# Last layer of a float32 kernel: two of three output tiles by Strassen's scheme, weights stationary

## The chip, the cores and the metric

The kernel runs on one core of a Trainium2 chip. The metric is device time of one execution in microseconds (us), the median of several runs. The engines are named as in the profile: PE (TensorE matmuls), PEld (its weight loads), DVE (VectorE), ACT (ScalarE), POOL (GpSimd), SP (the queue that issues most DMAs).

## The reference

```python
def _moe_ref(x, w1, w2, w3, w_out):
    a = x @ w1
    b = x @ w2
    h = a * b @ w3
    return (h @ w_out).astype(np.float32)
...
def _moe2_ref(x, w_in, w_out):
    h = x @ w_in
    relu6 = np.clip(h + 3.0, 0.0, 6.0)
    g = h * relu6 / 6.0
    return (g @ w_out).astype(np.float32)
...
    attn_out = _attn_ref(**attn_kwargs)
    x = attn_out.transpose(0, 2, 1, 3).reshape(B * S, H * D)
    x = _moe_ref(x=x, **moe_kwargs)
    return _moe2_ref(x=x, **moe2_kwargs)
```

There are 3072 tokens. The width is 384, the first feed-forward part has 1024 hidden units, the second 2048. The attention part is a recurrence with a decaying state. The weights come in as 64-bit floats, the rest as 32-bit floats.

## The kernel before

The tokens go in NB = 6 blocks of TB = 512. Attention units of two heads each come first and run beside the first feed-forward part; its w3 and w_out are folded into one matrix ahead of time, so that it has two layers. Call the products with w1 and w2 layer 1 (`l1_a`, `l1_b`, L720 to L734), the folded product layer 2 (`l2`, L737), the product with w_in layer 3 (`l3`, L804) and the product with the last w_out layer 4 (`l4`, L830).

Every large product is made of three float32r matmuls (`mm3`, L153 to L156): each operand is split into a rounded part hi and a remainder lo, and the sum is hi·hi + hi·lo + lo·hi. `split` (L149) makes the two parts: a copy on ACT (L150), a subtraction on POOL (L151).

In layers 3 and 4 the loop `steps2` runs over 6 blocks and, in each, over NM2 = 16 tiles m of 128 hidden units: 96 steps. A step issues on PE nine matmuls of layer 3 for tile m, 512 tokens moving (weights of w_in stationary), and then twelve of layer 4 for the tile before: for each of NC = 4 groups of 128 tokens, three matmuls with the tokens stationary and the 384 outputs moving, added into four PSUM banks over the block's 16 tiles. Between them stands the activation: DVE makes t = max(h+3, 0) (L811) and g = min(t, 6)·h (L817), ACT copies g to ghi (L150), POOL subtracts to glo (L151). At a block's end the four banks are scaled by 1/6 and written out as rows of 384 (L866, L870, L874).

The weights of layers 3 and 4 are read as 64-bit words and converted to 32 bits by a stream (`ws2`): two ACT instructions (L77, L78) and two DVE instructions (L85, L89) for a tile of 128x384, then `split`. `CONV` and `CONV2` say how many tiles are converted in each step: before, 18 in the last nine steps of layers 1 and 2, the rest one per step in the first block of layer 3. `u`, the first of the two words, lies in PSUM in the first part (`ws2.banks`) and in SBUF afterwards.

A check on alpha (`load_dev`, `deviate`, `make_flag`, `flag_sum`) is spread over some steps; its flag decides whether a general path runs at the end, which it doesn't here.

Up to step 46 of layers 1 and 2 a scheduler orders the instructions; from there (`MANUAL_FROM`) each engine runs them in the order of the code.

## Time and profile before

| | |
|---|---|
| median of 3 runs (range) | 880.73 us (879.99 to 882.34) |
| the profiled execution's own time | 878.07 us |
| its span, first to last instruction | 876.3 us |
| PE busy | 858.2 us (98% of the span), 6206 matmuls |
| DVE, ACT, POOL busy | 463.7, 344.5, 372.4 us |
| mean granted TensorE clock | 0.998 |

The first layer-3 matmul starts at 462.2 us, the last layer-4 matmul at 867.9 us: nearly half of the span is the stage that the change rewrites. A busy PE counts matmuls whose recorded times overlap; the pace is read from the distance between starts.

### The profile page before, as it was taken

To read this page: it belongs to the slowest core of one execution; us is meant where nothing else is said; L and a number is where in the kernel's file an instruction comes from. 1 tells how busy PE (TensorE), PEld (TensorE's weight loads), DVE (VectorE), ACT (ScalarE), POOL (GpSimd) and SP (SyncE) were. 2 spreads that over 40 slices of the span, in tenths; PEclk is the share of its full clock that TensorE was granted. 3 is DMA by queue.
4 is the path that set the end of the run, shared out by engine and by line. 5 is a ranking of instruction groups with operands and counts; after the bars stand their busy time and mean duration, and the time that the engine had idled before them with its cause. 6 is when DMAs were issued, how large, how long until landed. Compare 5 with 4: busy or idle time off the path is not lost.

```text
span 876.3 us, 16309 instructions
## 1 busy us (share of the span) xinstructions
PE 858.2 (98%) x6206; PEld 733.3 (84%) x6206; DVE 463.7 (53%) x838; ACT 344.5 (39%) x760; POOL 372.4 (42%) x388
## 2 busy tenths in 40 slices
PE   6999999999999999999999999999999999999996
PEld 5777888888888888888788999999899999999995
DVE  6787767887776767623426563333333333333332
ACT  4777776333322332326735465444221122121111
POOL 1445546334443334356545573342253243343231
PEclk9999999999999999999999999999999999999999
DMA  8896564376354443105523334022001001001001
GB/s 201 229 234 198 146 176 91 50 126 93 59 100 67 94 62 60 55 21 190 179 58 126 128 112 141 1 76 70 1 12 61 1 13 61 1 13 37 0 1 41
DMA packets 185127, 74.18 MB, mean 85 GB/s; under 512 B 154704, under 2 KB 173520, under 8 KB 185040
## 3 DMA queue, kind: packets, MB, share of 16 engines
q1 hardware_dynamic: 182336, 69.70, 32.4%
q0 software_dynamic: 2560, 3.15, 1.3%
q8 instruction: 51, 0.84, 0.4%
q14 instruction: 36, 0.29, 0.1%
q10 hardware_dynamic: 144, 0.20, 0.1%
HBM read 58.85 MB, written 9.44 MB: 78 GB/s over the span
## 4 chain that ended last, share of the span: by engine, by line
PE 93%; DMA 2%; ACT 1%; DVE 1%; issue 1%; POOL 0%; SPq 0%; POOLq 0%; DVEq 0%; ACTq 0%
PE acc L843 23%; PE h L154 8%; PE h L155 8%; PE h L156 7%; PE w L154 7%; PE w L156 7%; PE w L155 7%; PE acc L743 4%; PE acc L744 4%; PE acc L746 4%; PE sc L371 2%; PE facc L154 1%; PE facc L156 1%; PE facc L155 1%; PE py L458 1%
## 5 line engine op out<-in xcount | busy, mean ns | idle before, releaser
L151 POOL TENSOR_TENSOR glo<-g,ghi 128x512 fp32r<-128x512 f32 x95 | 125.7, 1323 | 234.0 <-ACT ghi L150 231.1
L811 DVE TENSOR_SCALAR t<-h 128x512 f32<-128x512 f32 x96 | 66.4, 692 | 232.3 <-PE h L156 232.3
L150 ACT CAST ghi<-g 128x512 fp32r<-128x512 f32 x95 | 59.0, 621 | 274.1 <-DVE g L817 252.8
L843 PE MATMUL acc<-wo2hi,ghi 128*128 128x384 f32 x384 | 130.3, 339 | 0.0
L843 PE MATMUL acc<-wo2lo,ghi 128*128 128x384 f32 x384 | 130.1, 339 | 0.0
L151 POOL TENSOR_TENSOR ablo<-ab,abhi 128x512 fp32r<-128x512 f32 x48 | 63.9, 1332 | 129.6 <-ACT abhi L150 129.5
L154 PE MATMUL w<-xhi,w 128*128 128x512 f32 x288 | 115.1, 401 | 1.6 <-ACT asb L723 1.4
L155 PE MATMUL h<-ylo,wihi 128*128 128x512 f32 x288 | 113.9, 395 | 0.0
L154 PE MATMUL h<-yhi,wihi 128*128 128x512 f32 x288 | 113.7, 395 | 0.0
L156 PE MATMUL w<-xhi,w 128*128 128x512 f32 x288 | 113.1, 393 | 0.0
L155 PE MATMUL w<-xlo,w 128*128 128x512 f32 x288 | 112.5, 391 | 0.0
L156 PE MATMUL h<-yhi,wilo 128*128 128x512 f32 x288 | 111.9, 388 | 0.0
L843 PE MATMUL acc<-wo2hi,glo 128*128 128x384 f32 x384 | 83.7, 339 | 0.0
L843 PEld LDWEIGHTS acc<-wo2hi,ghi 128*128 128x128 f32 x384 | 72.0, 188 | 5.1 <-ACT yt L756 0.8
L843 PEld LDWEIGHTS acc<-wo2lo,ghi 128*128 128x128 f32 x384 | 72.0, 188 | 3.5
L85 DVE SCALAR_TENSOR_TENSOR w<-u,w 128x384 uint32<-128x384 uint32 (+1 forms) x72 | 51.9, 724 | 40.5 <-ACT w L78 23.8
L817 DVE SCALAR_TENSOR_TENSOR g<-t,h 128x512 f32<-128x512 f32 x96 | 66.0, 688 | 9.9 <-POOL glo L151 0.2
L843 PEld LDWEIGHTS acc<-wo2hi,glo 128*128 128x128 f32 x384 | 69.1, 188 | 0.0
L154 PEld LDWEIGHTS w<-xhi,w 128*128 128x128 f32 x288 | 54.1, 188 | 14.2 <-ACT asb L723 1.8
L156 PEld LDWEIGHTS h<-yhi,wilo 128*128 128x128 f32 x288 | 54.1, 188 | 12.8
L156 PEld LDWEIGHTS w<-xhi,w 128*128 128x128 f32 x288 | 54.1, 188 | 11.6
L155 PEld LDWEIGHTS w<-xlo,w 128*128 128x128 f32 x288 | 54.1, 188 | 10.3
(131 smaller groups left out, 1507.7 us busy)
## 6 DMA issues: line engine op xcount, KB each, us to landing
raw<-in_moe_w_out SPq DMA_DIRECT2D x24, 384.0 KB, 3.3
raw<-in_moe_w SPq DMA_DIRECT2D x16, 512.0 KB, 4.9
raw<-in_moe_w SPq DMA_DIRECT2D x16, 384.0 KB, 3.5
raw<-in_moe_w_in SPq DMA_DIRECT2D x16, 384.0 KB, 3.7
y<-yt SPq DMA_DIRECT2D x18, 256.0 KB, 3.5
yraw<-y SPq DMA_DIRECT2D x18, 256.0 KB, 2.8
dev<-in_alpha SPq DMA_DIRECT2D x24, 192.0 KB, 3.7
out<-ot SPq DMA_DIRECT2D x23, 192.0 KB, 2.0
```

The source lines that it names most:

```text
L85: nc.vector.scalar_tensor_tensor(out=low, in0=u.bitcast(U32), scalar=3, in1=low, op0=ALU.logical_shift_left, op1=ALU.bitwise_or,)
L150: nc.scalar.copy(out=hi, in_=x)
L151: nc.gpsimd.tensor_tensor(out=lo, in0=x, in1=hi.bitcast(F32), op=ALU.subtract)
L154: nc.tensor.matmul(out=dst, lhsT=lh, rhs=rh, start=start, stop=False)
L155: nc.tensor.matmul(out=dst, lhsT=lh, rhs=rl, start=False, stop=False)
L156: nc.tensor.matmul(out=dst, lhsT=ll, rhs=rh, start=False, stop=stop)
L743: nc.tensor.matmul(out=acc1[o], lhsT=wh[:, sl], rhs=hi, start=m == 0, stop=False)
L744: nc.tensor.matmul(out=acc1[o], lhsT=wl[:, sl], rhs=hi, start=False, stop=False)
L746: nc.tensor.matmul(out=acc1[o], lhsT=wh[:, o * P:(o + 1) * P], rhs=lo, start=False, stop=m == NM1 - 1)
L811: nc.vector.tensor_scalar(out=t, in0=ps, scalar1=3.0, scalar2=0.0, op0=ALU.add, op1=ALU.max)
L817: nc.vector.scalar_tensor_tensor(out=g, in0=t, scalar=6.0, in1=ps, op0=ALU.min, op1=ALU.mult)
L843: nc.tensor.matmul(out=acc2[o], lhsT=x[:, o * P:(o + 1) * P], rhs=y, start=m == 0 and x is hi and y is wh, stop=stop,)
```

## The change

Layer 4 is done for pairs of tiles m. For outputs 0 to 255 (two tiles of 128) a pair's contraction (two tiles of 128), the two output tiles and the two halves of 256 tokens make a 2x2 by 2x2 product, done with seven products of blocks instead of eight. The third output tile (`o0`, `o1`) stays as it was. Weights are now stationary and tokens move: 256 columns in the seven products, 512 in the third tile. A pair issues on PE 7·3 matmuls of 256 columns and 2·3 of 512, where two steps before issued 24 of 384. The sums and differences of weights are made once (`pair_ops`); those of tokens are made in each pair (`operands`), with the subtraction for lo on DVE, and the combination of the seven sums into outputs once a block (`drain`). The outputs lie with output units on partitions, so that they are turned: on DVE in 32x32 blocks, and written in pieces of 128 bytes (`put_out`), in the last block on PE (`put_last`). The activation's first half goes from DVE to ACT as a Relu with bias 3. Conversion is moved: 26 weight tiles in the last nine steps of layers 1 and 2, six later, and five are loaded earlier. The check on alpha is taken later and more widely spaced.

```diff
-CONV = (2, 2, 2, 2, 2, 2, 2, 2, 2, 0)
-CONV2 = (0, 1)
+CONV = (5, 4, 3, 3, 3, 3, 3, 2, 0, 0)
+CONV2 = (0, 1, 1, 0, 0, 0, 0, 1, 1, 1, 1)
+HT = TB // 2
+NPAIR = NM2 // 2
+FIRST = (3, 6, 4, 7)
+SECOND = (2, 1, 5)
+PLACE = {3: (0, 0), 6: (0, 1), 4: (1, 0), 7: (1, 1), 2: (2, 0), 1: (2, 1), 5: (3, 0)}
+ONPOOL = ()
+DRAIN = ({2: (2, 1)}, {0: (3,), 1: (5, 0)})
+PUT = {3: 2, 4: 0, 5: 1}
...
+    def pair_ops(p, x0, x1):
...
+        nc.vector.tensor_tensor(
+            out=de[:, 0:2].rearrange("p o n -> p (o n)"), in0=col(x1, 0, 2), in1=col(x0, 0, 2), op=ALU.subtract
+        )
+        nc.vector.tensor_tensor(out=de[:, 2], in0=col(x0, 0), in1=col(x0, 1), op=ALU.add)
+        nc.vector.tensor_tensor(out=de[:, 3], in0=col(x1, 0), in1=col(x1, 1), op=ALU.add)
+        nc.vector.tensor_tensor(out=de[:, 4], in0=col(x0, 0), in1=col(x1, 1), op=ALU.add)
...
+            split(t[:, :, 0], t[:, :, 1], src)
...
+            (0, (4, 3, 6), de[:, 0:3]), (1, (7, 1), de[:, 3:5]),
+            (2, (5, "o1"), x1[:, P:].rearrange("p (o n) -> p o n", o=2)),
+            (3, (2, "o0"), x0.rearrange("p (o n) -> p o n", o=3)[:, ::2]),
...
+        g = ph2.tile([P, TB], F32, tag="g", name="g", bufs=2)
+        nc.scalar.activation(out=g, in_=ps, func=AF.Relu, bias=three)
+        nc.vector.scalar_tensor_tensor(out=g, in0=g, scalar=6.0, in1=ps, op0=ALU.min, op1=ALU.mult)
+        gs[j, m] = g
+
+    def operands(j, m):
...
+        nc.vector.tensor_tensor(out=d, in0=g[:, HT:], in1=g[:, :HT], op=ALU.subtract)
...
+            nc.vector.tensor_tensor(out=sm, in0=g0, in1=g, op=ALU.add)
...
+            nc.vector.tensor_tensor(out=cr, in0=g0[:, :HT], in1=g[:, HT:], op=ALU.add)
...
+        for k, hi, lo, x in todo:
+            nc.scalar.copy(out=hi, in_=x)
+        for k, hi, lo, x in todo:
+            eng = nc.gpsimd if k in ONPOOL else nc.vector
+            eng.tensor_tensor(out=lo, in0=x, in1=hi.bitcast(F32), op=ALU.subtract)
...
+        if what == 0:
+            mm(b[:, 0], hi, (p, half) == (0, 0) and k != "o1", False)
+            mm(b[:, 1], hi, False, False)
         else:
+            mm(b[:, 0], lo, False, p == NPAIR - 1)
...
+    def l4a(p, then=None):
+        for k in FIRST + ("o0",):
+            prod(p, k, 0)
...
+        for k in FIRST + ("o0",):
+            prod(p, k, 1)
+
+    def l4b(p, groups=(SECOND + ("o1",),)):
+        for ks in groups:
+            for what in range(2):
+                for k in ks:
+                    prod(p, k, what)
...
+            scaled(oth["m3"], 3, -1)
+            scaled(oth["m4"], 4, 1)
+            gather(1, 1, 6, 1, oth["m3"])
+            gather(0, 0, 7, -1, oth["m4"])
+        elif what == 5:
+            gather(1, 0, 5, 1, oth["m3"])
+            gather(0, 0, 5, -1)
+        elif what == 2:
+            gather(0, 1, 2, 1, oth["m4"])
+            gather(1, 1, 2, -1)
+        elif what == 1:
+            gather(0, 0, 1, 1)
+            gather(1, 1, 1, 1)
         else:
...
+            scaled(oth[2], "o1", 1)
...
+        nc.vector.transpose(out=t, in_=x)
...
+    def put_last(j, cs_):
+        for c in cs_:
+            ps = ps_mm.tile([P, DM], F32, tag="mm", name="oT")
+            for o in range(KD):
+                nc.tensor.transpose(ps[:, o * P:(o + 1) * P], oth[o][:, c * P:(c + 1) * P], ident)
+            t = raw2.tile([P, DM], F32, tag="raw", name="ot", bufs=RAW2)
+            if c % 2:
+                nc.vector.tensor_copy(out=t, in_=ps)
+            else:
+                nc.scalar.copy(out=t, in_=ps)
...
+        jp, mp = divmod(j * NPAIR + m // 2 - 1, NPAIR)
+        if jp >= 0:
+            if m % 2:
+                l4b(mp)
+            else:
+                l4a(mp, flag_sum if si == FLAG + 2 else None)
+        if j:
+            for what in DRAIN[0].get(m, ()):
+                drain(j - 1, what)
+            if m in PUT:
+                put_out(j - 1, PUT[m])
+        operands(j, m)
+        chore(CHORES)
+        if j:
+            for what in DRAIN[1].get(m, ()):
+                drain(j - 1, what)
...
+    l4a(NPAIR - 1)
+    drain(NB - 1, 3)
+    l4b(NPAIR - 1, ((2, 1), ("o1", 5)))
+    for what in (0, 2, 1, 5):
+        drain(NB - 1, what)
+    put_last(NB - 1, range(NC // 2, NC))
+    put_last(NB - 1, range(NC // 2))
```

PE in the middle of the stage. Before, layer 4 of one tile, behind nine matmuls of layer 3 (`acc` are the four token groups):

```order
L843 MATMUL acc_6113<-wo2hi,ghi 128x384
L843 MATMUL acc_6113<-wo2lo,ghi 128x384
L843 MATMUL acc_6114<-wo2hi,ghi 128x384
L843 MATMUL acc_6114<-wo2lo,ghi 128x384
...
L843 MATMUL acc_6115<-wo2hi,glo 128x384
L843 MATMUL acc_6116<-wo2hi,glo 128x384
```

PE of the changed kernel, the first half of layer 4 of a pair (`l4a`) and, behind nine matmuls of layer 3, its second half (`l4b`); m_6306, m_6311, m_6351 and m_6356 are banks of the seven sums, m_6316 is the third output tile, `bop` the prepared weights:

```order
L952 MATMUL m_6306<-ghi,bop 128x256 x2
L952 MATMUL m_6306<-dd,bop 128x256 x2
L952 MATMUL m_6311<-ghi,bop 128x256 x2
L952 MATMUL m_6311<-dd,bop 128x256 x2
L952 MATMUL m_6316<-ghi,bop 128x512 x2
L952 MATMUL m_6306<-glo,bop 128x256
...
L952 MATMUL m_6351<-shi,bop 128x256 x2
L952 MATMUL m_6351<-cross,bop 128x256 x2
L952 MATMUL m_6356<-shi,bop 128x256 x2
L952 MATMUL m_6316<-ghi,bop 128x512 x2
L952 MATMUL m_6351<-slo,bop 128x256
```

All products with hi stand ahead of all with lo in each half, and the operands of the second half (`shi`, `cross`) are asked for one layer-3 tile later than those of the first.

DVE of the changed kernel, two steps in the middle of a block, where two steps before had four instructions (t, g, t, g); d is the difference of a tile's two token halves, sm the sum of the pair's two tiles, cr the sum of one half of each:

```order
L899 SCALAR_TENSOR_TENSOR g<-g,h 128x512
L910 TENSOR_TENSOR d<-g 128x256
L932 TENSOR_TENSOR glo<-g,ghi 128x512
L932 TENSOR_TENSOR dd<-d,dd 128x256
L899 SCALAR_TENSOR_TENSOR g<-g,h 128x512
L910 TENSOR_TENSOR d<-g 128x256
L918 TENSOR_TENSOR sm<-g 128x512
L922 TENSOR_TENSOR cr<-g 128x256
L932 TENSOR_TENSOR glo<-g,ghi 128x512
L932 TENSOR_TENSOR dd<-d,dd 128x256
L932 TENSOR_TENSOR slo<-sm,shi 128x512
L932 TENSOR_TENSOR cross<-cr,cross 128x256
```

Twelve instructions stand in two steps, and the four remainders of an odd tile are the last work ahead of the next tile's g.

## Rows read from the trace of the kernel before

**Rows 1.** The page: busy times of the engines, PE and its clock in 40 slices.

```profile
PE 858.2 (98%) x6206; PEld 733.3 (84%) x6206; DVE 463.7 (53%) x838; ACT 344.5 (39%) x760; POOL 372.4 (42%) x388
...
PE   6999999999999999999999999999999999999996
...
PEclk9999999999999999999999999999999999999999
```

**Rows 2.** Waits of PE: who, for whom, us in total, times, longest.

```profile
PE aT L313 <- DMA al<-in_alpha: 4.4, 1, 4.4
PE kb L406 <- DVE KT L360: 2.4, 1, 2.4
PE w L154 <- ACT asb L723: 1.4, 1, 1.4
```

**Rows 3.** Busy time by windows: stretch, length, PE, PEld, DVE, ACT, POOL, clock, DMA.

```profile
407.00:462.00 55.00, 53.59 (x237) 44.06 (x236) 21.58 (x39) 32.73 (x68) 30.61 (x29) 1.00 0.44 135
462.00:868.00 406.00, 405.97 (x2029) 367.06 (x2027) 157.44 (x233) 124.98 (x250) 163.05 (x128) 1.00 0.14 45
```

**Rows 4.** Timeline of PE, one step: start, length, what.

```profile
702.24 0.40 PE L154 MATMUL h<-yhi,wihi 128*128 128x512 f32 x1
...
704.32 0.34 PE L843 MATMUL acc<-wo2hi,ghi 128*128 128x384 f32 x1
...
706.44 0.40 PE L154 MATMUL h<-yhi,wihi 128*128 128x512 f32 x1
```

**Rows 5.** Timeline of PE, the first steps of the stage.

```profile
462.18 0.39 PE L154 MATMUL h<-yhi,wihi 128*128 128x512 f32 x1
...
464.22 0.39 PE L743 MATMUL acc<-abhi,w34hi 128*128 128x512 f32 x1
...
466.26 0.39 PE L154 MATMUL h<-yhi,wihi 128*128 128x512 f32 x1
...
470.99 0.39 PE L154 MATMUL h<-yhi,wihi 128*128 128x512 f32 x1
```

**Rows 6.** Groups by line of PEld, layer 4: count, busy us, mean ns.

```profile
L843 PEld LDWEIGHTS acc<-wo2hi,ghi 128*128 128x128 f32 x384 | 72.0, 188 | 5.1 <-ACT yt L756 0.8
```

**Rows 7.** Timeline of PEld where two loads meet no running float32r matmul.

```profile
290.81 0.19 PEld L743 LDWEIGHTS acc<-abhi,w34hi 128*128 128x128 f32 x1
290.92 0.19 PEld L744 LDWEIGHTS acc<-abhi,w34lo 128*128 128x128 f32 x1
```

**Rows 8.** Groups by line and form of DVE and ACT: durations by size.

```profile
L817 DVE SCALAR_TENSOR_TENSOR g<-t,h 128x512 f32<-128x512 f32 x96 | 66.0, 688 | 9.9 <-POOL glo L151 0.2
L524 DVE TENSOR_TENSOR A<-sb,low 128x256 f32<-128x256 f32 x32 | 11.2, 392 | 5.6 <-PE sb L518 5.6
L307 DVE STREAM_TRANSPOSE kT<-kn 128x512 f32<-128x512 f32 x15 | 10.3, 686 | 0.0
L824 DVE TENSOR_TENSOR glo<-g,ghi 128x512 fp32r<-128x512 f32 x1 | 0.7, 693 | 0.7 <-ACT ghi L823 0.7
L150 ACT CAST ghi<-g 128x512 fp32r<-128x512 f32 x95 | 59.0, 621 | 274.1 <-DVE g L817 252.8 <-PE acc L843 15.4 <-DVE flag L901 3.6
```

**Rows 9.** Timeline of DVE, t and g of one step.

```profile
704.52 0.69 DVE L811 TENSOR_SCALAR t<-h 128x512 f32<-128x512 f32 x1 [2.72 <-PE h L156]
705.31 0.69 DVE L817 SCALAR_TENSOR_TENSOR g<-t,h 128x512 f32<-128x512 f32 x1
```

**Rows 10.** Groups by line of POOL from 405 to 463 us.

```profile
L151 POOL TENSOR_TENSOR ablo<-ab,abhi 128x512 fp32r<-128x512 f32 x10 | 13.0, 1297 | 19.1 <-ACT abhi L150 19.1
L151 POOL TENSOR_TENSOR wilo<-w,wihi 128x384 fp32r<-128x384 f32 x11 | 11.2, 1025 | 9.5 <-ACT wihi L150 9.4
```

**Rows 11.** Timeline of DVE and POOL around 463 us.

```profile
461.63 0.56 DVE L89 SCALAR_TENSOR_TENSOR w<-u,w 128x384 uint32<-128x384 uint32 x1
...
463.12 2.32 POOL L151 TENSOR_TENSOR wilo<-w,wihi 128x384 fp32r<-128x384 f32 x2
...
463.13 1.43 DVE L85 SCALAR_TENSOR_TENSOR w<-u,w 128x384 uint32<-128x384 uint32 x1 [0.94 <-ACT w L78]
```

**Rows 12.** Timeline of the end, and four transposes on PE earlier.

```profile
115.94 0.60 PE L683 MATMUL w3ps<-cs,w 128*128 128x128 f32 x4
...
867.78 0.49 ACT L870 ACTIVATE ot<-acc 128x384 f32<-128x384 f32 x1 [0.57 <-PE acc L843]
867.94 0.33 PE L843 MATMUL acc<-wo2hi,glo 128*128 128x384 f32 x1
...
868.31 0.56 DVE L866 TENSOR_SCALAR ot<-acc 128x384 f32<-128x384 f32 x1 [0.50 <-PE acc L843]
```

More of the change, by code (lines that the diff above doesn't have):

```diff
@@ L144, in attn_moe_kernel @@
     nc.gpsimd.memset(adev, -ADEV * ADEV)
+    three = const.tile([P, 1], F32, tag="three", name="three")
+    nc.gpsimd.memset(three, 3.0)
     over = const.tile([P, NDEV], F32, tag="over", name="over")
@@ L165, in __init__ @@
             self.banks = []
+            self.spare = None
+            self.sent = self.made = 0
         def issue(self, count=1):
@@ L184, in prep @@
                         u = cv.tile([P, n], F32, tag="u", name="u", bufs=UB)
-                    w = cv.tile([P, math.prod(shape[1:])], F32, tag="w", name="w", bufs=WB)
+                    pl, bufs = cv, WB
+                    if self.spare and self.made < SPARED and self.made % (WB + 1) == WB:
+                        pl, bufs = self.spare, 1
+                    self.made += 1
+                    w = pl.tile([P, math.prod(shape[1:])], F32, tag="w", name="w", bufs=bufs)
                     f64_prep(nc, raw, u, w)
@@ L787, in attn_moe_kernel, with chore @@
+    chores = []
+    spread = []
+    def chore(n):
+        for _ in range(min(n, len(chores))):
+            f, *args = chores.pop(0)
+            f(*args)
     yraw = {}
@@ new lines, in attn_moe_kernel, with region, prod, mm @@
+    acc2 = {}
+    oth = {}
+    def region(k):
+        if k in PLACE:
+            i, half = PLACE[k]
+            return acc2[i][:, half * HT:(half + 1) * HT]
+        return acc2[4]
+    def prod(p, k, what):
+        i, half = PLACE.get(k, (4, 0))
+        if (p, what, half) == (0, 0, 0) and k != "o1":
+            pl, tag = ((ps_mm2, "mm2a"), (ps_mm2, "mm2b"), (ps_acc, "acc0"), (ps_acc, "acc1"), (ps_acc, "acc2"))[i]
+            acc2[i] = pl.tile([P, TB], F32, tag=tag, name=f"m{i}", bufs=1)
+        hi, lo = aop[k]
+        b = bop[p, k]
+        def mm(x, y, start, stop):
+            nc.tensor.matmul(out=region(k), lhsT=x, rhs=y, start=start, stop=stop, skip_group_check=True)
+        if what == 0:
+            mm(b[:, 0], hi, (p, half) == (0, 0) and k != "o1", False)
+            mm(b[:, 1], hi, False, False)
+        else:
+            mm(b[:, 0], lo, False, p == NPAIR - 1)
@@ L817, in l3, with scaled, gather @@
+    SIXTH = 1.0 / 6.0
+    def scaled(dst, k, sign):
+        nc.scalar.activation(out=dst, in_=region(k), func=AF.Copy, scale=sign * SIXTH)
+    def gather(o, t, k, sign, base=None):
+        dst = oth[o][:, t * HT:(t + 1) * HT]
         nc.vector.scalar_tensor_tensor(
-            out=g, in0=t, scalar=6.0, in1=ps, op0=ALU.min, op1=ALU.mult
-        )
-        ghi = gpool.tile([P, TB], F32R, tag="abhi", name="ghi")
-        glo = gpool.tile([P, TB], F32R, tag="ablo", name="glo")
-        if last:
-            nc.scalar.copy(out=ghi, in_=g)
-            nc.vector.tensor_tensor(out=glo, in0=g, in1=ghi.bitcast(F32), op=ALU.subtract)
-        else:
-            split(ghi, glo, g)
@@ new lines, in gather @@
+            out=dst, in0=region(k), scalar=sign * SIXTH, in1=dst if base is None else base,
+            op0=ALU.mult, op1=ALU.add,
+        )
+    def l4a(p, then=None):
+        for k in FIRST + ("o0",):
+            prod(p, k, 0)
+        if then:
+            then()
+        for k in FIRST + ("o0",):
[5 more added lines that the diff above has]
+                    prod(p, k, what)
@@ new lines, in put_out @@
+    def put_out(j, o):
+        x = oth.pop(o)
+        t = raw2.tile([P, TB], F32, tag="raw", name="oT", bufs=RAW2)
+        nc.vector.transpose(out=t, in_=x)
+        t = blocks(t)
+        for c, n, b, t0 in spans(j):
+            rows = out[b * S + t0:b * S + t0 + n * P, :].rearrange("(t r) d -> r t d", r=Q32)
+            for a in range(P // Q32):
+                d0 = o * P + a * Q32
+                nc.sync.dma_start(
+                    out=rows[:, :, d0:d0 + Q32],
+                    in_=t[a * Q32:(a + 1) * Q32, c * (P // Q32):(c + n) * (P // Q32), :],
+                )
@@ L898, in flag_sum @@
     def flag_sum():
-        pf = ps_mm2.tile([P, 2], F32, tag="mm2", name="pf")
-        nc.tensor.matmul(out=pf[:1, :1], lhsT=far[:, 1:2], rhs=ones[:, 0:1], start=True, stop=True)
-        nc.vector.tensor_copy(out=flag, in_=pf[:1, :1])
+        pf = ps_mm2.tile([P, TB], F32, tag="acc3", name="pf")[:1, :1]
+        nc.tensor.matmul(out=pf, lhsT=far[:, 1:2], rhs=ones[:, 0:1], start=True, stop=True)
+        nc.scalar.copy(out=flag, in_=pf)
     def w3_items(f):
@@ L971, in attn_moe_kernel @@
         if si == n1:
+            spare.close()
+            ph2 = pool(main, "ph2", 1)
             l3(*steps2[0])
```

251 lines of the change are left out of this document (140 added, 111 removed).

## The prediction, made blind

> **What bounds the kernel now.** I read the page first, then the waits of PE, the windows, and the timeline of one step. PE is busy in all but the first of 40 slices at the full clock level, 2.4 GHz, and its waits add up to some 10 us in three large pieces, all of them early [rows 1, 2]. So the kernel is as long as PE's list of work, and a change pays if it shortens that list without making PE wait. In the stage of layers 3 and 4, 462 to 868 us, PE is busy 405.97 of 406.00 us, while DVE has work for 157, ACT for 125 and POOL for 163 [rows 3]: there is room on DVE and ACT, and the change uses it.
>
> The pace of PE is the distance between starts, not the printed length. One step is 4.20 us (702.24 to 706.44): nine matmuls of 512 columns take 2.08, 231 ns each, and twelve of 384 take 2.12, 176.8 ns each [rows 4]. The difference is 54.2 ns for 128 columns, near the 53.3 that 128 columns take at 2.4 GHz, so some 15 ns a matmul do not depend on the columns. At the stage's start nine of the same 512-column matmuls took 2.04 us, 226.7 ns each [rows 5].
>
> **The change, part by part.** The times are against the profiled execution, 878.07 us with a span of 876.3.
>
> *Layer 4 on PE.* A pair of tiles costs now 24·176.8 = 4.243 us. It will cost 21 matmuls of 256 columns and 6 of 512. No row has a float32r matmul of 256 columns. Taking the column step once more off, 176.8 − 54.2 = 122.6 ns; the pair is 21·0.1226 + 6·0.231 = 3.961 us, 0.282 less, and 48 pairs make −13.6 us. The bounds are the weight load's. From below: two loads that meet no running float32r matmul follow each other after 0.11 us [rows 7], so a matmul with its own load is not paced under some 111 ns: −0.25 us a pair more, −25 us in all. From above: a load is printed with 188 ns [rows 6]; if the next matmul waited for that, a pair would cost 5.33 us, +52 us. I take 122.6: the 384-column matmuls already start 176.8 ns apart, under the 188 of the load between them, so the printed length is not a barrier, and 122.6 is still above 111.
>
> A rule speaks against the change here. The Trainium skill, page "TensorE: Matmul & The Clock Gate", section "The mechanism", says that a weight load overlaps matmuls in flight only where the row groups differ; all loads here use all rows. By that a 256-column matmul would cost its stream and a load of 107 ns (same page, "LDWEIGHTS (loading the stationary operand)"), well over 200 ns, and the stage would get longer by some 80 us, an estimate. The trace disagrees: 384 columns are 160 ns at 2.4 GHz and start 176.8 ns apart with a load each [rows 4], which leaves no room for a load in series.
>
> *DVE in a pair.* From the code it has twelve instructions: six of 512 columns at 0.69 us (two g, the sum, three remainders; the remainder's own row is 693 ns) and six of 256 at 0.392 [rows 8]: 6.49 us of a pair's 18·0.231 + 3.961 = 8.12. On PE this costs nothing while it is covered. What covers it: the remainders glo and dd of an odd tile are asked for by the second pass of `l4a`, which starts after nine layer-3 matmuls (2.08) and ten of the first pass (1.44), so 3.5 us after `l4b` let their buffers go; they need 1.1 us of DVE, so DVE may be 2.4 us late before PE waits. ACT does two Relus, three casts of 512 (0.621 each) and three of 256; at 0.69 or less each this is under 5 us of 8.12.
>
> *Combining a block's sums.* For five blocks DVE has eight more instructions of 256 columns and three transposes of 512 (0.686): 8·0.392 + 3·0.686 = 5.2 us [rows 8], within the next block's steps 0 to 5. Two pairs have 2·1.63 = 3.3 us to spare, so DVE falls back by 1.9, less than the 2.4 above. A block as a whole is covered (57.1 of 64.9 us). I take 0.2 us a block, 1 us in all; the bounds are 0 and 5·1.9 = 9.5. The outputs' many small writes go through SP's queue in the next block's first steps, ahead of that block's y loads, which are wanted three steps later: nothing.
>
> *The last block.* Nothing follows to cover it. Now the last matmul starts at 867.94, DVE starts on its output 0.37 later and is done after 0.56 [rows 12]. In its place come, behind the last product, two DVE instructions of 256 (0.70 at the pitch that overlaps their ends), three transposes at 0.11 (four took 0.60 with the last one's end [rows 12]), a copy of 0.5, and the same again for the second two groups, as only two PSUM banks hold transposed tiles: 0.37 + 0.70 + 2·(0.33 + 0.2 + 0.5) + 0.5, some 3.6 us in place of 0.93: +2.7. The last pair's operands come with no pair of work between: +0.5 (0 to 1.5).
>
> *Conversion moved.* From 407 us on POOL will do, by the order of the changed program, 14 splits of w_in, 6 of three and 18 of two tiles of prepared weights, ten ablo, one xlo, three ylo: at 1.025 and 1.297 us, and 0.75 for 256 columns by the same slope [rows 10], 52 us, in the 58 us until layer 2 asks for the last ablo. Then there are 24 sums and differences of weights on DVE, each with two SBUF operands. Where DVE ran such an instruction beside a POOL subtraction it took 1.43 us, not 0.56 [rows 11]; if POOL in turn is held for theirs (0.28 us on average), POOL comes to 59 us. So PE will wait in this stretch, for ablo or asb: 1 us at least, and with POOL's idle time of today (9.5 us behind wilo's casts [rows 10]) 10 at most. I take the middle, 5.4, less the 1.4 that PE waits there today [rows 2]: +4. The page "SBUF — State Buffer" of the Trainium skill, section "SBUF: two separate sides", says that VectorE instructions with two SBUF inputs and GpSimd lock each other out for a whole instruction; the row of 1.43 us agrees.
>
> *The first block.* Now the second step takes 4.73 us instead of 4.20 [rows 5]. Six weight tiles and the pipeline's filling remain: +0.5 (0 to 3).
>
> Sum: −13.6 + 1 + 2.7 + 0.5 + 4 + 0.5 = −4.9, so 873.2 us for the profiled execution. That one was 2.7 us under the median of its three runs; for the median this is 880.73 − 4.9 = 875.8 us, in round numbers **876**. About 0.3%, 2.6 us, is what a measurement of this kernel can tell from no change.
>
> **The rivals.**
>
> *The short matmul is cheaper.* If the stage ran as at its start, 226.7 ns for 512 columns and 118 for 256, a pair of steps would cost 7.92 us in place of 8.40: −22.8 + 8.7 = −14, 867 us. For: the first nine matmuls of the stage ran so [rows 5]. Against: every later step is at 231.
>
> *The weight load sets the pace (slower).* It has 111 of 122.6 ns. Each nanosecond over the latter costs 21·48 = 1.0 us, so at 127.5 ns the gain is gone, and from 130 the change is measurably slower. If the matmul gets no shorter than the 384-column one, 176.8 ns, it is 930 us. For: the margin is 11 ns, and today's matmuls show 15 ns that do not belong to columns. Against: 384 and 512 differ by what their columns take, so no load binds at 384.
>
> *DVE becomes the bound (slower).* If every instruction also waits 0.10 us for the one before, as g does behind t (0.79 from start to start, 0.69 long [rows 9]), a pair costs 7.69 us, five blocks with their 6.3 us more overrun by 2.9 us each, the first with its conversions by 5: +20 in place of 1.5, 894 us. It decides from some 7.5 us a pair. Against: most of the twelve do not depend on their neighbour.
>
> *The conversion stretch is worse.* With 10 to 14 us of waiting it is 881 to 886.
>
> **How the numbers follow.** My forecast 0.47, with its own range 869 to 883; cheaper matmul 0.15; load as the pace 0.15; DVE 0.10; conversion 0.13. Faster by over 0.3% (under 878.1): 0.36 + 0.15 + 0.01 = 0.52. Within: 0.10 + 0.05 + 0.01 = 0.16. Slower: 0.32. The range leaves out the load's case and a little of DVE's and goes from 863, a little under the cheaper matmul, to 893.
>
> **What would show it.** In the changed profile, starts of 256-column matmuls 122 to 124 ns apart and PE busy through the stage would bear out the main term; 130 or more refutes it. Waits of layer 4 for glo, dd, slo or cross on DVE would be the DVE rival; waits of layer 1 or 2 for asb or ablo between 407 and 466 us the conversion. The end should show about 3.6 us from the last product to the last copy. The forecast is wrong if PE waits in most pairs, or if the pace of layer 3 changes too.

## The result and the profile after

| | before | after |
|---|---|---|
| median (range), us | 880.4 (879.99 to 882.34) | 866.7 (865.26 to 870.25) |
| ratio, 95% interval | | 0.985 (0.982 to 0.989) |
| profiled execution, its span, us | 878.07, 876.3 | 870.25, 868.4 |
| mean granted clock | 0.998 | 0.991 |

The changed kernel is faster by 1.5%, 13.7 us in the medians, where 4.9 were forecast. The two profiled executions are only 7.8 us apart, and the trace tells why. PE's page rows of the changed kernel (to be read against [rows 1]):

```profile
PE 847.0 (98%) x6362; PEld 708.4 (82%) x6362; DVE 662.2 (76%) x1310; ACT 485.0 (56%) x1068; POOL 258.8 (30%) x310
...
PE   6999999999999999999899999999999999999996
...
PEclk9999999999999999999999999999999999999998
```

DVE has 662 us of work in place of 464, PE 11 us less. Three stretches of this execution ran at half the clock, 1.2 GHz. The windows around them (stretch, length, PE busy, clock, DMA share, GB/s):

```profile
27.00:30.40 3.40, 3.40 (x29) 0.51 1.03 246
143.10:146.50 3.40, 3.40 (x13) 0.50 0.01 1
433.30:436.70 3.40, 3.40 (x10) 0.50 0.67 233
```

Each costs half of its length, 1.7 us. The first two lie ahead of the stretches that were rewritten, and ahead of the early loads of weights, which are issued from 147.3 us on. A matmul of layer 1 that the kernel before starts at 405.40 us starts here at 408.61, so 3.2 us of this execution's time are counted apart from the change. `fourth_buffer`, with the same instructions there, had neither of the two stretches; whether the change makes them likelier is not shown. The kernel before had no such stretch in its profiled execution until PE's work was over.

Now the waits of PE in the changed kernel, against [rows 2]:

```profile
PE aT L340 <- DMA al<-in_alpha: 4.5, 1, 4.5
PE w L169 <- DVE ab L756: 2.9, 2, 2.4
...
PE m L952 <- ACT dd L929: 0.8, 2, 0.6
```

New are the two waits of layer 1 behind `ab` (1.4 us behind `asb` before) and small ones of layer 4 for its operands, in the first block. The windows, as in [rows 3] (PE, PEld, DVE, ACT, POOL, clock, DMA share, GB/s):

```profile
407.00:469.00 62.00, 59.08 (x252) 48.07 (x251) 45.71 (x80) 47.93 (x108) 49.19 (x50) 0.97 0.49 156
...
509.00:535.00 26.00, 24.92 (x133) 20.89 (x132) 23.88 (x47) 16.10 (x35) 7.13 (x7) 1.00 0.01 2
535.00:850.00 315.00, 315.00 (x1781) 275.74 (x1780) 266.16 (x534) 202.90 (x417) 15.50 (x12) 1.00 0.18 39
```

From 535 to 850 us PE is never idle, with DVE at 266 of 315 us. One pair of steps in that stretch, to be read against [rows 4] (start, length, what; x2 is two instructions in one row):

```profile
558.87 0.40 PE L169 MATMUL h<-yhi,wihi 128*128 128x512 f32 x1
...
560.93 0.40 PE L952 MATMUL m<-ghi,bop 128*128 128x256 f32 x2
561.16 0.40 PE L952 MATMUL m<-dd,bop 128*128 128x256 f32 x2
...
563.03 0.39 PE L169 MATMUL h<-yhi,wihi 128*128 128x512 f32 x1
...
565.07 0.40 PE L952 MATMUL m<-shi,bop 128*128 128x256 f32 x2
...
566.82 0.40 PE L169 MATMUL h<-yhi,wihi 128*128 128x512 f32 x1
```

Two 256-column matmuls start every 0.23 to 0.24 us; of the 815 neighbours of that size 791 are less than 130 ns apart, that is outside waits, and their mean distance is 117.6 ns. Layer 3 takes 2.06 and 2.04 us, and the pair 7.95 in place of 8.40. A whole block of eight pairs shows it with all that recurs in one, combining and transposes included:

```profile
547.12 0.39 PE L169 MATMUL h<-yhi,wihi 128*128 128x512 f32 x1
...
610.89 0.39 PE L169 MATMUL h<-yhi,wihi 128*128 128x512 f32 x1
```

That is 63.77 us for eight pairs, 7.97 each. With 48 pairs and the other places, the account of the two profiled executions is:

| place | forecast, us | trace, us | read from |
|---|---|---|---|
| pairs of steps | -13.6 | -20.6 | 48·(8.40 - 7.97) |
| combining | +1 | 0 | PE idle 0 from 535 to 850; one step is longer by 0.3 beside the flag's matmul, as one was before (622.15 to 626.66) |
| conversion stretch | +4 | +3.4 | stage starts at 468.83 (462.18 before), less 3.2 from earlier |
| first block | +0.5 | +3.7 | four first passes of layer 4 longer by 1.2, 1.9, 0.4, 0.7, less 0.5 of before [rows 5] |
| last pair's operands | +0.5 | +0.7 | its first pass took 2.75 us, not 2.10 |
| the end | +2.7 | +1.5 | last product to end of span 9.87 us, 8.36 before [rows 12] |
| half clock and waits before 407 us | | +3.2 | 408.61 against 405.40 |
| sum | -4.9 | -8.1 | 870.25 - 878.07 = -7.8; a hundredth in the pair's difference is worth 0.5 |

The 7.8 and the 3.2 counted apart give the change 11.0 us. The medians are 13.7 apart: the 7.8 of these two executions, the 2.3 by which that of before is under its median, and the 3.5 by which that of after is over its own. So 2.7 of the 13.7 lie in no place of the table.

### The profile page after: what moved, and what is told of

The parts are those of the page before. It is cut to its first block, busy times and chain, and to the rows that moved or that the text cites. A ratio compares the mean times of both kernels' runs of the same rounds, so it can differ in the third digit from the quotient of the medians.

```text
span 868.4 us, 17489 instructions
## 1 busy us (share of the span) xinstructions
PE 847.0 (98%) x6362; PEld 708.4 (82%) x6362; DVE 662.2 (76%) x1310; ACT 485.0 (56%) x1068; POOL 258.8 (30%) x310
## 4 chain that ended last, share of the span: by engine, by line
PE 77%; DVE 4%; ACT 3%; DMA 1%; issue 1%; POOL 1%; DVEq 0%; ACTq 0%
PE m L952 21%; PE h L169 7%; PE h L170 7%; PE h L171 7%; PE w L169 6%; PE w L171 6%; PE w L170 6%; PE acc L770 3%; PE acc L771 3%; PE acc L773 3%; DVE w L98 1%; PE sb L614 1%; PE sb L563 1%; PE sb L572 1%; PE sb L545 1%
## 5 line engine op out<-in xcount | busy, mean ns | idle before, releaser
L952 PE MATMUL m<-ghi,bop 128*128 128x512 f32 (+1 forms) x384 | 98.9, 339 | 0.6 <-ACT ghi L929 0.4
L899 DVE SCALAR_TENSOR_TENSOR g<-g,h 128x512 f32<-128x512 f32 x96 | 65.7, 684 | 44.3 <-ACT g L898 44.0
L166 POOL TENSOR_TENSOR ylo<-yraw,yhi 128x512 fp32r<-128x512 f32 x18 | 23.5, 1305 | 240.7 <-ACT yhi L165 240.7
L898 ACT ACTIVATE g<-h,three 128x512 f32<-128x512 f32 x96 | 65.9, 686 | 48.7 <-PE h L171 48.3
L932 DVE TENSOR_TENSOR glo<-g,ghi 128x512 fp32r<-128x512 f32 x96 | 69.3, 722 | 13.3 <-ACT ghi L929 13.3
L952 PEld LDWEIGHTS m<-ghi,bop 128*128 128x128 f32 x384 | 62.4, 189 | 5.2 <-ACT ghi L929 1.1
L165 ACT CAST abhi<-ab 128x512 fp32r<-128x512 f32 x48 | 29.7, 620 | 63.9 <-DVE ab L756 63.9
L952 PE MATMUL m<-dd,bop 128*128 128x256 f32 x288 | 64.0, 284 | 0.8 <-ACT dd L929 0.8
L170 PEld LDWEIGHTS h<-ylo,wihi 128*128 128x128 f32 x288 | 54.1, 188 | 11.7
```

The lines of the kernel that those rows point to most:

```text
L165: nc.scalar.copy(out=hi, in_=x)
L166: nc.gpsimd.tensor_tensor(out=lo, in0=x, in1=hi.bitcast(F32), op=ALU.subtract)
L170: nc.tensor.matmul(out=dst, lhsT=lh, rhs=rl, start=False, stop=False)
L898: nc.scalar.activation(out=g, in_=ps, func=AF.Relu, bias=three)
L899: nc.vector.scalar_tensor_tensor(out=g, in0=g, scalar=6.0, in1=ps, op0=ALU.min, op1=ALU.mult)
L932: eng.tensor_tensor(out=lo, in0=x, in1=hi.bitcast(F32), op=ALU.subtract)
```

## The experiments

Twelve kernels ran. The times stand beside runs of the kernel before on the same chip, whose median was 879.6 to 879.9 us. The question was first why the pairs gained half as much again as forecast, and then what the three costs (conversion, first block, end) hang on.

| run | median, us | ratio to before (95%) |
|---|---|---|
| `columns` | 862.95, once | |
| `plain512` | 878.8 | 0.999 (0.997 to 1.002) |
| `places_swapped` | 880.8 | 1.002 (1.000 to 1.003) |
| `tokens_above` | 880.7 (one of ten: 2147) | 1.000 (0.997 to 1.002) |
| `more_dve` | 872.5 | 0.992 (0.991 to 0.994) |
| `fourth_buffer` | 865.7 | 0.985 (0.981 to 0.989) |
| `one_operand` | 865.9 | 0.985 (0.982 to 0.989) |
| `spread` | 866.5 | 0.986 (0.984 to 0.987) |
| `spread_late` | 863.5 | 0.980 (0.977 to 0.982) |
| `sums_half_pool` | 864.5 | 0.983 (0.980 to 0.986) |
| `fewer_early` | 868.6 | 0.988 (0.983 to 0.992) |
| `even_order` | 867.7 | 0.985 (0.982 to 0.989) |

### The price of a short matmul: `columns`

```
+COLS = (256, 240, 224, 192, 160, 128)
...
+        n = TB if k in ("o0", "o1") else HT if p == 0 else COLS[blk[0]]
...
-            nc.tensor.matmul(out=region(k), lhsT=x, rhs=y, ...)
+            nc.tensor.matmul(out=region(k)[:, :n], lhsT=x, rhs=y[:, :n], ...)
```

> The short products move 256, 240, 224, 192, 160 and 128 columns in blocks 0 to 5 (the first pair of each block keeps 256, so that every sum is set), 21 of them a pair as before; the columns left out make blocks 1 to 5 incomplete. Theory: a short matmul costs its columns plus some 11 ns until the weight load binds, and a load needs 0.11 us: starts 118, 112, then 110 to 111 in blocks 2 to 5; blocks 3 to 5 are no shorter than block 2. Rival 1, the load is no part of it: 118, 111, 104, 91, 78, 64, block 5 shorter than block 0 by 7 pairs times 21 times 54 ns = 7.9 us. Rival 2, the load is already the pace at 256: 118 in every block, no change of time.

A first pass of layer 4 in the last block, PE's timeline, now with 128 columns:

```profile
832.99 0.33 PE L956 MATMUL m<-ghi,bop 128*128 128x128 f32 x2
833.16 0.39 PE L956 MATMUL m<-dd,bop 128*128 128x128 f32 x2
...
835.03 0.40 PE L170 MATMUL h<-yhi,wihi 128*128 128x512 f32 x1
```

The pass takes 2.04 us; with 256 columns, above, it took 2.10 (560.93 to 563.03). Half the columns should have saved 12·53 = 640 ns and saved 60. With three matmuls of 512 at 227 ns taken off, the twelve short ones come to 118 ns each at 256 columns and 113 at 128. Single distances agree: the median is 112 ns at 240 and 224 columns, 111 at 192, 160 and 128. The mean is lower, 105 at 128 columns, since a short matmul behind a long one is followed after 58 ns; the next long one is then followed after 280 to 291 ns, not 227, so it is the loads that keep their pace. So a load of new weights every 111 to 113 ns is a floor, as the theory had it from [rows 7], and 256 columns stand 5 ns above it. Both rivals fall.

### The plain product with weights stationary: `plain512`

```
+    FULL = {3: "o0", 4: "o1", 2: "s", 5: "o1"}
...
+        if k in (6, 7, 1):
+            return
-        hi, lo = aop[k]
+        hi, lo = aop[FULL.get(k, k)]
...
-            nc.tensor.matmul(out=region(k), lhsT=x, rhs=y, ...)
+            nc.tensor.matmul(out=acc2[i], lhsT=x, rhs=y, ...)
```

> The same operands, waits and work on the other engines, but in place of the 21 products of 256 columns a pair has 12 more of 512 (18 in all), that is the plain product with weights stationary and tokens moving; the output is not the layer's. Theory: layer 3 is back at 227 ns because the matmuls of 384 columns with tokens stationary are gone, not because of the scheme: 512 columns start every 227 ns everywhere, a pair is 36 times 0.227 = 8.17 us in place of 7.95, and with 48 pairs the time is 10 us above the changed kernel, 876 to 878. Rival: the faster layer 3 needs the short products beside it; then all 36 run at 231, a pair is 8.32, and the time is 883 to 885.

The time, 878.8, fits the theory's 876 to 878 better than the rival's 883 to 885, but neither saw what the pace did. Layer 4 in two places of the run, PE's timeline, six matmuls in each first row:

```profile
566.53 1.56 PE L957 MATMUL m<-ghi,bop 128*128 128x512 f32 x6
567.93 0.86 PE L957 MATMUL m<-glo,bop 128*128 128x512 f32 x3
...
599.46 1.52 PE L957 MATMUL m<-ghi,bop 128*128 128x512 f32 x6
600.82 0.84 PE L957 MATMUL m<-glo,bop 128*128 128x512 f32 x3
```

Six starts take 1.40 us in the first (233 ns each) and 1.36 in the second (227), with the same instructions and the same moving tiles. What differs is where the prepared weights lie: those of pairs 0 to 4 in the upper pool, 183 to 229 KB of a partition (KB is 1000 bytes), those of pairs 5 to 7 in tiles that lie under 133 KB. In every block the steps of the first five pairs ran at 233.6 and those of the last three at 226.7. So in this run the pace goes with the place. This run also prices the scheme: without it, and with everything else of the change, the time is that of the kernel before.

### Is it the place: `places_swapped` and `tokens_above`

```
-            hi = wts.tile([P, KD, P], F32R, tag="wahi", name="wihi", bufs=2 * NM1)
+            hi = wi.tile([P, KD, P], F32R, tag=f"wihi{m}", name="wihi")
...
-            hi = wi.tile([P, DM], F32R, tag=f"wo2hi{m}", name="wo2hi")
+            hi = wts.tile([P, DM], F32R, tag="wahi", name="wo2hi", bufs=2 * NM1)
...
-                [wo2_item(m) for m in range(4)] + [wi2_item(m) for m in range(NM2 - 2)]
+                [wi2_item(m) for m in range(NM2 - 2)] + [wo2_item(m) for m in range(4)]
```

> The kernel before, with the prepared weights of layers 3 and 4 exchanged in SBUF: w_in's 32 tiles take the upper pool (180 to 229 KB of a partition), w_out's the lower tiles (21 to 70 KB) that layers 1 and 2 leave; the same matmuls in the same order. In the run with the plain product, 512 columns started every 233.6 ns with stationary tiles in the upper pool and every 226.7 with those of the lower tiles, same moving tiles. Theory: the 384-column matmuls of the kernel before (176.8 ns, and layer 3 at 231 behind them) pay the same, since weights and tokens both lie above 140 KB; with w_out below, 384 columns start every 173.3 ns and 512 every 226.7, a step is 4.12 us in place of 4.20, and the time falls by 95 times 0.08 = 7.6 us, 872 to 873 us. Rival: the excess belongs to 384-column matmuls with tokens stationary wherever their operands lie: steps stay at 4.20 us, 880 us.

One step of this version of the kernel before, PE's timeline:

```profile
701.79 0.34 PE L843 MATMUL acc<-wo2hi,ghi 128*128 128x384 f32 x1
...
702.14 0.33 PE L843 MATMUL acc<-wo2hi,ghi 128*128 128x384 f32 x1
...
703.88 0.39 PE L154 MATMUL h<-yhi,wihi 128*128 128x512 f32 x1
...
705.98 0.34 PE L843 MATMUL acc<-wo2hi,ghi 128*128 128x384 f32 x1
```

With `w_out` below, ten matmuls of 384 columns take 1.74 us from 702.14, 173.5 ns each, as the theory said (176.8 before). But layer 3, whose weights went above, now takes 2.10 us, 233.3 ns a matmul, and the step is 4.19 again. The expectation left out that layer 3's weights, which make room, now lie above. The time did not move; how the step divides did.

```
-        ghi = gpool.tile([P, TB], F32R, tag="abhi", name="ghi")
+        ghi = late.tile([P, TB], F32R, tag="abhi", name="ghi")
```

> The kernel before, same instructions in the same order; only the high and low part of g (layer 4's stationary tokens) lie at 161 to 169 KB of a partition in place of 147 to 155 KB, so on the side of w_out (180 to 229 KB). Theory: the pace is slower by 3.5 to 7 ns a matmul where one operand lies above some 155 KB and the other below, as weights above with tokens below (233.6), w_in above with y below (233.3) and now w_out above with g below (176.8); with both above, 384 columns start every 173.3 ns and layer 3 every 226.7, a step is 4.12 us and the time 7.6 us shorter, 872 to 873 us. Rival: any operand above 180 KB costs it, wherever the other lies: 4.20 us a step, 880 us.

```profile
704.79 0.40 PE L154 MATMUL h<-yhi,wihi 128*128 128x512 f32 x1
...
706.87 0.34 PE L843 MATMUL acc<-wo2hi,ghi 128*128 128x384 f32 x1
...
708.99 0.40 PE L154 MATMUL h<-yhi,wihi 128*128 128x512 f32 x1
```

2.08 and 2.12 us, as before: 176.7 ns for 384 columns. The theory of two sides falls, the rival stands: in these three runs weights in the upper pool went with 3.3 ns (moving, 384 columns) to 7 ns (stationary, 512 columns) more a matmul, for both places of the tokens that were tried.

The place alone is not the rule, however. The changed kernel has 512-column matmuls in layer 4 too, with their weights in the same two places as in `plain512`. One pair whose weights lie below, PE's timeline of the changed kernel:

```profile
601.74 0.63 PE L952 MATMUL m<-ghi,bop 128*128 128x512 f32 x2
602.21 0.28 PE L952 MATMUL m<-glo,bop 128*128 128x256 f32 x1
```

Two starts take 0.47 us, 235 ns each, where the same weights and tokens ran at 227 in `plain512`. Over the later five blocks the medians are 235 ns with weights below and 231 to 233 above, so here those below are the slower ones. Something else decides with the place, perhaps which matmuls stand beside each other; no run separates it. Why layer 3 with its weights below runs at 231 in the kernel before stays open too. A version with both sets of weights below was not tried; there is no room for it.

### How much cover DVE has: `more_dve`

```
+            nc.vector.tensor_tensor(out=sm, in0=g0, in1=g, op=ALU.add)
             todo += [("s", sh, sl, sm), ("c", cross[:, 0], cross[:, 1], cr)]
```

> The sum of the two tiles of a pair is computed twice, one more DVE instruction of 512 columns a pair (48 in all, 0.69 us each), which changes no value. Theory: DVE's 6.5 us of a pair's 7.95 are covered, so 7.2 are too, but a block with its 5.2 us of combining then has 62.8 of 63.6 us and falls behind at the block's start: a few waits of 1 to 2 us a block behind glo or dd, 3 to 8 us in all, 869 to 874. Rival 1, DVE was already close to the bound (the rival of the prediction): each instruction shows, 20 to 33 us. Rival 2, wholly covered: within 1 us.

872.5 us, 5.8 over the changed kernel, for 33 us of added DVE work: the time is the theory's, and both rivals fall. DVE's window:

```profile
535.00:850.00 315.00, 313.74 (x1766) 273.68 (x1766) 285.71 (x567) 198.96 (x413) 15.52 (x12) 1.00 0.18 39
```

Step by step, the first block is 3.1 us longer than in the changed kernel, 1.7 of it by a stretch at half the clock (509.5 to 512.9), and each later block 0.4 to 0.8, in its first pairs, where the sums of the block before are combined (a first pass of 2.65 in place of 2.10). Nearly all other pairs are unchanged. So the waits at the blocks' starts are smaller than the theory's 1 to 2 us, and over half of the loss lies in the first block, which it did not name. Away from conversions and combining DVE has over 0.69 us to spare in a pair of 7.97.

### The end: `fourth_buffer`

```
+            if c == 1:
+                t = xp.tile([P, TB], F32, tag="xflat", name="ot", bufs=2)[:, :DM]
```

> The last of the four output copies of the last block gets a buffer of its own. Theory: in the changed kernel its DVE copy waited 1.62 us for the output DMA of the first copy; now it starts right behind the transposes, and the end comes 1.4 to 1.6 us earlier, 865.1 us. Rival: the end is set by the output DMAs on the one queue, which then wait for each other: under 0.5 us.

The last copy, timelines of the changed kernel and then of this one:

```profile
858.53 0.28 PE L952 MATMUL m<-slo,bop 128*128 128x256 f32 x1
...
862.34 0.56 DVE L1029 COPY ot<-oT 128x384 f32<-128x384 f32 x1 [1.62 <-DMA out<-ot]
```

```profile
854.02 0.28 PE L952 MATMUL m<-slo,bop 128*128 128x256 f32 x1
...
856.91 0.56 DVE L1032 COPY ot<-oT 128x384 f32<-128x384 f32 x1 [0.70 <-PE oT L1026]
```

From the last product to the end of the last copy it is now 3.45 us, not 4.37, yet from there to the span's end the time is taken back: 9.68 us from last product to end (863.7 - 854.02), against 9.87. The rival stands: the output DMAs set the end. The last of them lands 7.63 us behind the last product in the changed kernel and 6.83 here, but 6.69 in `one_operand`, whose last copy ends as late (4.38 us) as the changed kernel's. The median is 1.0 us lower, too little to tell from no change.

### The conversion stretch: `one_operand`, `spread`, `spread_late`, `sums_half_pool`, `fewer_early`, `even_order`

The changed kernel's DVE in the stretch, by groups (count, busy us, mean ns, idle before), and the same four instructions later, when POOL has little to do:

```profile
L844 DVE TENSOR_TENSOR de<-w 128x256 f32<-128x256 f32 x6 | 4.6, 765 | 0.1
L848 DVE TENSOR_TENSOR de<-w 128x128 f32<-128x128 f32 x6 | 4.4, 736 | 0.0
...
L844 DVE TENSOR_TENSOR de<-w 128x256 f32<-128x256 f32 x1 | 0.4, 418 | 0.0
...
L848 DVE TENSOR_TENSOR de<-w 128x128 f32<-128x128 f32 x1 | 0.3, 283 | 0.0
```

Beside POOL's remainders a sum of 128 columns takes 736 ns on average and up to 1.37 us, without them 283. Ahead of the longer of PE's two waits (second fence), DVE's timeline has four such sums, of which two are shown, before the `ab` that layer 1 needs:

```profile
423.54 1.51 DVE L844 TENSOR_TENSOR de<-w 128x256 f32<-128x256 f32 x1
424.97 1.10 DVE L847 TENSOR_TENSOR de<-w 128x128 f32<-128x128 f32 x1
...
431.64 0.68 DVE L756 TENSOR_TENSOR ab<-w,asb 128x512 f32<-128x512 f32 x1
```

```profile
423.52 0.50 PE L169 MATMUL w<-xhi,w 128*128 128x512 f32 x1 [0.47 <-DVE ab L756]
432.38 0.50 PE L169 MATMUL w<-xhi,w 128*128 128x512 f32 x1 [2.44 <-DVE ab L756]
```

How the waits divide is not the kernel's alone. `columns`, `plain512` and `more_dve` have the same conversions, and their waits there were 1.2 to 1.5 us and then 1.2, not 0.5 and 2.4. In `columns` the first of the sums above took 0.41 us, not 1.51, which it took here with a remainder of POOL that had begun 0.08 us ahead of it (423.46). So a shift of this size between two single profiles is no effect of an edit.

First the lock:

```
-        nc.vector.tensor_tensor(out=de[:, 2], in0=col(x0, 0), in1=col(x0, 1), op=ALU.add)
+        nc.vector.tensor_scalar(out=de[:, 2], in0=col(x0, 0), scalar1=0.5, scalar2=None, op0=ALU.mult)
```

> The four sums and differences of a pair of weight tiles become four DVE instructions of the same shapes with one SBUF operand (a product with 0.5), so the prepared weights are not the scheme's. Theory: in the changed kernel DVE and POOL hold each other there; with one operand the rows of 256 fall from 765 ns to under 400 and those of 128 from 734 to 870 to under 300, the wait of layer 1 behind ab shrinks from 2.9 to under 1 us, and the stall of the first block (3 us) to under 1.5: 862 to 864 us in place of 866.7. Rival: the waits come from the amount of conversion, not from the lock: rows fall, waits stay within 0.5 us, 866 us.

```profile
L848 DVE TENSOR_SCALAR de<-w 128x128 f32<-128x128 f32 x5 | 3.6, 718 | 0.0
...
L844 DVE TENSOR_SCALAR de<-w 128x256 f32<-128x256 f32 x5 | 2.2, 443 | 0.6 <-POOL bop L166 0.6
```

Two of these products where nothing holds them, DVE's timeline:

```profile
457.31 0.28 DVE L844 TENSOR_SCALAR de<-w 128x256 f32<-128x256 f32 x1
...
457.64 0.22 DVE L848 TENSOR_SCALAR de<-w 128x128 f32<-128x128 f32 x1
```

Only part of the edit's aim was met: the rows of 256 fell to 443 ns, those of 128 stayed at 580 to 718, single ones up to 1.32 us. PE's waits were 2.2 us behind `ab` and 1.1 behind `asb`, no fewer than before. So one operand does not free DVE from POOL here. The page "SBUF — State Buffer" of the Trainium skill, section "SBUF: two separate sides", lets VectorE contend with GpSimd also in a mode that uses two ports. The rows agree with it, though none names the mode: left alone, a product takes 0.28 us for 256 columns and 0.22 for 128, a sum 0.42 and 0.28, so 128 columns more cost a product about half of what they cost a sum. If so, the edit changed how DVE takes the lock and not whether, and it is no test of the theory. What the lock costs PE stays open.

Then the order and the amount (the runs from here have the fourth buffer too):

```
spread:
-CONV = (5, 4, 3, 3, 3, 3, 3, 2, 0, 0)
+CONV = (3, 3, 3, 3, 3, 3, 3, 3, 2, 0)
-CONV2 = (0, 1, 1, 0, 0, 0, 0, 1, 1, 1, 1)
+CONV2 = (0, 1, 1, 0, 0, 1, 0, 1, 0, 1, 0, 1)
spread_late: CONV2 as in spread, CONV unchanged
sums_half_pool: as spread_late, and
+        eng = nc.gpsimd if p % 2 else nc.vector
fewer_early:
+CONV = (4, 3, 3, 3, 3, 3, 3, 2, 0, 0)
+CONV2 = (0, 1, 1, 0, 1, 1, 0, 1, 1, 0, 1, 1)
even_order: as fewer_early, CONV = (3, 3, 3, 3, 3, 3, 3, 3, 0, 0), and
+ORDER2 = "o0 o1 i0 i1 o2 o3 i2 i3 o4 o5 i4 i5 o6 i6 o7 i7 ..."
```

> Weight tiles are converted three a step from the start in place of 5, 4, 3 and so on, those of the first block at steps 5, 7, 9, 11 in place of 7 to 10; also the buffer of the run before for the last copy. Theory: layer 1's waits behind ab (2.9 us) and the first block's stalls (3 us) come from bunches of conversions in the fixed order of DVE ahead of ab, g and d; spread they shrink to under 1.5 us each, and the time is 862 to 863.5 us in place of 865.7. Rival: DVE has too little time in the stretch in all (26 conversions at 1.1 us, 6 pairs' sums at 3.5 and nine ab at 0.69 are 56 us of 57), so the waits only come later in it: 865 to 867.

The waits behind `ab` stayed (2.8 us, 2.5 the longest), and as conversions ran late into the stage, its first pair waited 2.0 us and ran 3.4 us at half the clock. The later stalls of the first block were gone. The rival is right for the stretch, the theory for the block.

> The changed kernel's conversions up to the stage's start, and only those of the first block spread (steps 5, 7, 9, 11 in place of 7 to 10), with the buffer for the last copy. Theory: the first block's stalls at its fifth, sixth and seventh pair (3 us) go, as in the run with both spread, and the first steps stay as in the changed kernel: 862.5 to 864 us. Rival: DVE's arrears only move to the first pairs: 865 to 866.5.

The fifth pair's step in the changed kernel and then in this one, starts of layer 3:

```profile
508.01 0.40 PE L169 MATMUL h<-yhi,wihi 128*128 128x512 f32 x1
...
514.11 0.39 PE L169 MATMUL h<-yhi,wihi 128*128 128x512 f32 x1
```

```profile
510.99 0.40 PE L169 MATMUL h<-yhi,wihi 128*128 128x512 f32 x1
...
515.19 0.40 PE L169 MATMUL h<-yhi,wihi 128*128 128x512 f32 x1
```

6.10 us became 4.20; over the block 2.45 us came back, in the trace the same matmul after it stands 0.05 us from the changed kernel's where it had stood 2.50 behind it. The theory holds, and at 863.5 us (0.980) this is by its median the fastest version of the study that computes the whole layer.

> As the run with the first block's conversions spread, and the four sums and differences of every second pair of weight tiles are POOL's in place of DVE's (POOL is busy 49 of 62 us in the stretch, DVE 46 with 3.5 us a pair). Theory: DVE's chain ahead of ab is what layer 1 waits for, so without every second pair's sums the waits (2.9 us) and the half clock behind them (1.7 us lost) go: 859 to 861.5 us. Rival: POOL's own queue, with ablo and the remainders of the weights behind the sums, then is late by as much: 863 to 866.

Layer 1's waits behind `ab` fell to 1.0 us and no half clock followed, so PE, counted from the stretch's start, was 3.1 us ahead of the changed kernel in mid-stretch; but the stage's first matmul then waited 2.2 us behind `asb`, and at its start 2.6 of the 3.1 were gone. The rival's time is right, and the arrears move; that it is POOL which is late is not shown, since PE waited for ACT.

> Two conversions less in the last steps of layers 1 and 2 (24 in place of 26, the first step 4 in place of 5) and eight in the first block, at steps 1, 2, 4, 5, 7, 8, 10, 11; with the buffer for the last copy. Theory: the 2.4 us wait of layer 1 behind ab comes from the five and four conversions at the start of the stretch; with one less in each it shrinks to under 1.5 us and no half clock follows, while the first block takes two more, +1 us at most: 861.5 to 863 us, against 863.5 with the first block spread alone. Rival: the 2.4 us are those of one pair's sums on DVE (four instructions, 5 us), so the wait stays and the first block adds to it: 864 to 865.5.

> As the run with fewer conversions, three a step, and the order of the weight tiles evened out, so that no step has the sums of more than one pair of w_out's tiles. Theory: DVE has 3 times 1.1, 3.5 for a pair's sums and 0.69 for ab, 7.5 us in a step with a pair and 4.0 in one without, against 6.1 us of PE, so it falls back by under 1.5 us and catches up: the waits of layer 1 shrink to under 1 us, the time is 860.5 to 862.5. Rival: ACT and POOL, which take part in each conversion, hold DVE up as before: waits of 2 us and more, 863.5 to 865.

Neither theory of the two held. With fewer early conversions the waits were 1.5 and 1.2 us, 2.7 in all, and no half clock followed, as in `columns`, `plain512` and `more_dve` without the edit; with the even order they were 1.9 us behind `asb`. In both, the two conversions more cost the first block some 3.4 us against `spread_late`: the first passes of its fourth and fifth pair took 3.5 us in place of 2.1. Read together, the runs speak for DVE, ACT and POOL having too little time from 407 to 520 us for the work, so that what is taken from one stretch is paid in the next; no run shows which of the three would have to be faster.

## Why the prediction was right and where it was off

**The sign and the reason held.** PE set the pace, its list got shorter, and the other engines' additions were covered from 535 us on. The time lies in the range. By the account above the change gave 11.0 us where 4.9 were forecast: 7.0 more in the pairs, 0.6 less in all the rest, and 0.3 that the table does not place. That the median lies in the range owes much to its lower end, which was set by a rival. One of the prediction's own signs of being wrong came true: the pace of layer 3 changed too, from 231 to 228 ns.

**The step that failed is a size**, "Taking the column step once more off, 176.8 − 54.2 = 122.6 ns", and with it the six matmuls and layer 3 at 231. Measured are 117.6 for the short ones, and 7.97 - 21·0.1176 = 5.50 us for the pair's 24 long ones, 229 each. The first is worth 21·5.0 ns·48 = 5.0 us, the second 2.0: the 7 us that were missed. `places_swapped` shows a part of the 5.0 ns: with `w_out` elsewhere the same 384 columns ran at 173.5, and from this and the 226.7 of the stage's start [rows 5] the same subtraction gives 120.3. So 2.3 of the 5.0 were in the rows that were subtracted; the other 2.7 stay open. The rival of the cheaper matmul, at 0.15, had 226.7 and 118 and hit the median (867), in part by luck: its pair is 7.92 where 7.97 was measured, and 2.7 of the medians' 13.7 lie in no place of the account. "Every later step is at 231" was no argument against it, since all those steps stood beside matmuls of 384 columns, which the change removes; in `plain512`, without them, layer 3 took 227 to 228 ns.

**The weight load** was bounded rightly: the floor is 111 to 113 ns, 5 ns under what 256 columns take, so it neither sets the pace (rival at 0.15) nor gives more to a shorter one. The page "TensorE: Matmul & The Clock Gate" of the Trainium skill gives columns over 1.2 in "LDWEIGHTS (loading the stationary operand)", an estimate of 107 ns for 128; the floor is 4 to 6 above it. The same page of the Trainium skill says in "The mechanism" that loads overlap matmuls only between different row groups; the 117.6 ns here are against it, since 107 for the columns and a load in series would not fit.

**DVE in a pair and the combining** cost nothing, where 0 and 1 us had been costed: DVE is busy 266 of 315 us from 535 us on, and PE never waits there. The rival with DVE as the bound (894) falls: `more_dve` shows that even 0.69 us more a pair is covered outside the blocks' starts and the first block.

**The conversion stretch** was right in size, +3.4 for +4, but partly by luck. The price was worked out from POOL's arrears, with PE waiting for ablo or asb; PE waited for `ab`, which DVE makes, and 1.7 of the 3.4 is a half-clock stretch behind the 2.44 us wait, which was not foreseen.

**The first block** was too low, 0.5 (0 to 3) for 3.7. The step "Six weight tiles and the pipeline's filling remain" counted conversions but not that four of them stood in four successive steps, ahead of `d` in DVE's order. One of their rows there took 1.65 us (505.51), beside a remainder that POOL had begun at 505.45; in `spread_late` each took 0.54 to 0.56. `spread_late` took 2.45 of it back by spacing them alone.

**The end** was 1.5, not 2.7, because the output DMAs, not the copies, set it; the last copy itself ended 4.37 us behind the last product, not 3.6, as it waited for a buffer.

## What to carry to other kernels

Before a price is worked out by subtracting rows, look whether the same instruction runs at another pace elsewhere in the trace: beside the 231 of the steps stood the 226.7 of the stage's start, and an experiment found 173.5 for the 176.8. Such a difference can go away with the change. A matmul with new weights each time has a floor of some 111 ns here, so halving columns pays down to 256 and hardly below. One profile of each version does not tell apart waits of a microsecond or two: look first how much they move in runs whose code is the same there. Work that is added on engines beside the bound is free only where they have time in every stretch: here DVE's load rose from 157 us in 406 [rows 3] to 266 in 315 and cost nothing in the long stage, but the conversions cost some 7 us in the 115 us around its start, and there spacing them out (2.45 us) was what paid.
